# A linear-attention and gated-MLP kernel: features turned by transposing DMAs, key-value sums kept in PSUM, q and k weights read from DRAM turned

## The chip, the cores and the metric

The kernel runs on one core of one Trainium2 chip. The metric is device time in microseconds (us) of one execution; lower is better. The engines are TensorE (PE in the rows; its weight loads are PEld), VectorE (DVE), ScalarE (ACT), GpSimd (POOL) and SyncE (SP), which here only issues DMAs.

## The reference

A token matrix x of 2048 x 512 is normalised, and two branches of the normalised xn are added to x. Branch A is linear attention with 32 heads of 16 features; phi is a softmax of w_phi's product and a softmax of its negative, side by side.

```
xn = (x - mean) / sqrt(var + 1e-5)
q, k, v = split(xn @ wqkv)                       # 32 heads of 16
pq, pk = q @ w_phi, k @ w_phi                    # per head, 16 x 16
phi = concat(softmax(p), softmax(-p))            # 32 features a head, of pq and of pk
kv, z = sum_s phi_k * v, sum_s phi_k             # per head
A = ((phi_q @ kv) / (phi_q @ z + 1e-6)) @ wo
B = ((xn @ w_gate) * (xn @ w_up)) @ w_down       # inner width 1792
out = x + A + B
```

## The kernel before

Tokens are worked in 16 tiles of 128. The weights and x are loaded at the start by SP's queue, whole matrix by whole matrix (lines 347 to 364); w_phi's 16 KB come by GpSimd's queue. `wprime_steps` folds w_phi into the q and k weights: f1 turns a 128-column block of wq or wk with four TensorE transposes (matmuls by the identity, line 323, evicted by ScalarE, line 287), f2 multiplies it by the block-diagonal `wbd` that GpSimd builds (line 395).

Then three stages. **Opening**: per four tiles, normalisation statistics (DVE line 432, and nine tiny GpSimd operations for the inverse root, lines 448 to 455), per tile `emit_xn` (line 465) and `emit_xT`, four TensorE transposes. **k stage**, per tile: `k_stage1` makes k's features and v (eight matmuls of 512 columns, line 309; exponentials by ScalarE), `k_stage2` sums each head (line 499), takes reciprocals (line 504) and scales both halves (line 506, one on DVE, one on GpSimd) into an array of all 16 tiles; gate and up products of 5 of the 14 inner blocks go in between (`emit_glu_up`, 512 columns at a time). `emit_kv` then sums the key-value products over all tiles, 128 matmuls of 129 columns. **q stage**, per tile: `q_stage1` makes the features, `q_stage2a` turns them (eight TensorE transposes), multiplies them by the key-value sums (eight matmuls of 128 columns) and by z (eight of 8 columns); `q_stage2b` divides on DVE, `q_stage2b_pe` turns the result (four transposes). `final_chunks` fills in the other 9 inner blocks (256 columns at a time, lines 674, 675 and 679), the down and wo products (line 654), and adds x by a matmul with the identity.

Each operation is a step with its reads and writes; `_emit_all` orders all engines' steps by a list schedule over assumed costs, and each engine then runs its list in that order, waiting on semaphores. In these lines the q stage is paced:

```
    for t in range(NT):
        q_stage2b(t)
        if t + 2 < NT:
            q_stage1(t + 2)
        emit_c(1)
        if t + 1 < NT:
            q_stage2a(t + 1)
        emit_c(1)
        q_stage2b_pe(t)
        done_2b[0] = t
        emit_c(2)
```

Of the kernel before, what the change touches and what calls it, by code (L numbers as in the profile page):

```python
# [5 lines left out]
BF16 = mybir.dt.bfloat16  # L6
# [4 lines left out]
I32 = mybir.dt.int32  # L11
# [3 lines left out]
S_TOK = 2048  # L15
D = 512
H = 32
DH = 16
# [4 lines left out]
FT_EARLY = 5  # L23


def _ap_intervals(ap, max_n=64):
    esz = mybir.dt.size(ap.dtype)
    off = ap.offset
    pairs = [tuple(pr) for pr in list(ap.ap)[1:] if pr[1] > 1]
    inner_hi = 0  # L30
    rest = []
    for step, cnt in pairs:
        if step == 1:
            inner_hi = max(inner_hi, cnt - 1)
        else:
            rest.append((step, cnt))
    total = 1
    for step, cnt in rest:
        total *= cnt
    if total > max_n:  # L40
        lo, hi = 0, inner_hi
        for step, cnt in rest:
            if step > 0:
                hi += step * (cnt - 1)
            else:
                lo += step * (cnt - 1)
        return [((off + lo) * esz, (off + hi + 1) * esz)]
    outs = []
    for n in range(total):
        base = off  # L50
        m = n
        for step, cnt in rest:
            base += step * (m % cnt)
            m //= cnt
        outs.append((base * esz, (base + inner_hi + 1) * esz))
    return outs


class _Step:
# [3 lines left out]
    def __init__(self, eng, fn, idx, lane):  # L63
# [10 lines left out]
        self.cost = 100.0  # L74
        self.seq = 0
        self.finish = 0.0


class _Sched:

    def __init__(self, nc):
        self.nc = nc
        self.steps = []
        self.by_eng = {PE: [], ACT: [], DVE: [], POOL: [], SP: []}
        self.regions = {}
        self.dma_count = 0
        self.allow_overwrite = False

    def _overlaps(self, space, lo, hi):
        out = []  # L90
        for reg in self.regions.setdefault(space, []):
            if reg[0] < hi and lo < reg[1]:
                out.append(reg)
        return out

    def _record(self, st, reads, writes):
        deps = []
        for ap in reads:
            space = str(ap.tensor.name)
            ivs = _ap_intervals(ap)  # L100
            if space == "ps":
                ivs = sorted(set((lo // 2048 * 2048, (hi + 2047) // 2048 * 2048) for lo, hi in ivs))
            for lo, hi in ivs:
                regs = self._overlaps(space, lo, hi)
                for reg in regs:
                    if reg[2] is not None and reg[2] is not st:
                        deps.append(reg[2])
                    reg[3].append(st)
                if not regs:
                    self.regions[space].append([lo, hi, None, [st]])  # L110
        for ap in writes:
            space = str(ap.tensor.name)
            for lo, hi in _ap_intervals(ap):
                new_regions = []
                for reg in self._overlaps(space, lo, hi):
                    if reg[2] is not None and reg[2] is not st and not reg[3] and not self.allow_overwrite:
                        raise RuntimeError(
                            f"step {st.idx} ({st.eng}) overwrites unread data in {space}[{reg[0]}:{reg[1]}] "
                            f"written by step {reg[2].idx} ({reg[2].eng})")
                    if reg[2] is not None and reg[2] is not st:  # L120
                        deps.append(reg[2])
                    for r in reg[3]:
                        if r is not st:
                            deps.append(r)
                    if reg[0] < lo:
                        new_regions.append([reg[0], lo, reg[2], list(reg[3])])
                    if reg[1] > hi:
                        new_regions.append([hi, reg[1], reg[2], list(reg[3])])
                    self.regions[space].remove(reg)
                self.regions[space].extend(new_regions)  # L130
                self.regions[space].append([lo, hi, st, []])
        seen = set()
        dd = []
        for d in deps:
            if id(d) not in seen:
                seen.add(id(d))
                dd.append(d)
        st.deps = dd

    def step(self, eng, fn, reads=(), writes=(), cost=None):  # L140
        st = _Step(eng, fn, len(self.steps), eng)
        self.steps.append(st)
        self.by_eng[eng].append(st)
        reads = list(reads)
        writes = list(writes)
        self._record(st, reads, writes)
        if cost is None:
            n = 1
            for ap in writes + reads:
                try:  # L150
                    n = max(n, ap.free_size())
                except Exception:
                    pass
            if eng == ACT:
                cost = 230.0 + 0.84 * n
            elif eng == DVE:
                cost = 130.0 + 1.0 * n
            elif eng == POOL:
                cost = 250.0 + 2.2 * n
            else:  # L160
                cost = 100.0 + 0.45 * n
        st.cost = cost
        return st

    def dma(self, eng, out_ap, in_ap, is_out=False, reads=None, writes=None):
        nc = self.nc
        lane = ("dma", self.dma_count)
        self.dma_count += 1
        holder = {}

        def fn(e):
            ins = e.dma_start(out_ap, in_ap)
            return ins
# [34 lines left out]
def _build(nc, es, A_x, A_wqkv, A_w_phi, A_wo, B_w_gate, B_w_up, B_w_down, out):  # L208
# [3 lines left out]
    def alloc(name, nelem_bf16, at=None):  # L212
# [724 lines left out]
```

## Time and profile before

| | |
|---|---|
| three runs | 271.51 us (median), 270.52, 272.21 |
| profiled execution, first to last instruction | 270.5 us |
| TensorE busy | 246.2 us, 91% |
| VectorE, ScalarE, GpSimd busy | 156.2, 128.1, 53.8 us |
| DMA | 12.12 MB, most of it in the first 31 us |

The profile gives no time of its execution beside the span; the median of the runs is 1.0 us above the span. An engine's busy time counts overlapping matmuls by their modelled ends, so TensorE's share says where it had work queued, not that it ran at its best rate.

### The profile page before, as it was taken

The numbers are of one execution on the slowest core, as the hardware profiler recorded it, in microseconds if no ns is written. First come the engines' busy times: TensorE is split into PE (matmuls) and PEld (weight loads), VectorE is DVE, ScalarE is ACT, GpSimd is POOL, SyncE is SP. The second block draws the span as 40 slices with busy tenths as digits, with TensorE's granted clock in tenths as the row PEclk, the third lists the DMA queues.
The fourth block names the chain that finished last, engine by engine and source line by source line (L and its number), as shares of the span: only waits on it lengthen the run. The fifth ranks groups of instructions, "written<-read, shape, count | busy, mean of one in ns | idle before, by whom it ended". The sixth has DMA issues, their size and how long they took to land.

```text
span 270.5 us, 4879 instructions
## 1 busy us (share of the span) xinstructions
PE 246.2 (91%) x1902; PEld 156.7 (58%) x1936; DVE 156.2 (58%) x364; ACT 128.1 (47%) x261; POOL 53.8 (20%) x99
## 2 busy tenths in 40 slices
PE   0068999999999999999999999999999999999994
PEld 0046544444444587777567765775766757566661
DVE  3951699989797985787677776542232323313231
ACT  1057898646665704776665755632222313222221
POOL 4560253333442430313112131100000000000000
PEclk9999999999999999999999999999999999999999
DMA  6999300000000000000000001001001010000101
GB/s 198 351 393 381 119 0 1 2 0 0 0 0 2 0 4 2 0 2 0 22 19 2 4 1 41 0 2 39 0 2 39 2 39 0 26 15 2 39 1 39
DMA packets 9446, 12.12 MB, mean 45 GB/s; under 512 B 448, under 2 KB 8400, under 8 KB 9424
## 3 DMA queue, kind: packets, MB, share of 16 engines
q1 hardware_dynamic: 9392, 11.80, 12.6%
q8 instruction: 15, 0.25, 0.4%
q0 software_dynamic: 32, 0.02, 0.1%
q14 instruction: 7, 0.06, 0.1%
HBM read 9.72 MB, written 2.10 MB: 44 GB/s over the span
## 4 chain that ended last, share of the span: by engine, by line
PE 80%; DVE 8%; ACT 3%; DMA 3%; issue 3%; POOL 2%; DVEq 0%; POOLq 0%
PE ps L309 50%; PE ps L654 24%; PE ps L323 7%; ACT arena L287 3%; DMA arena<-in_A_w_phi_dram 3%; DVE arena L499 2%; DVE arena L506 1%; DVE arena L534 1%; DVE arena L504 1%; POOL arena L395 1%; DVE arena L465 1%; DVE arena L576 0%; DVE arena L679 0%; DVE arena L457 0%; POOL arena L449 0%
## 5 line engine op out<-in xcount | busy, mean ns | idle before, releaser
L287 ACT ACTIVATE arena<-ps 128x512 bf16<-128x512 f32 (+1 forms) x260 | 126.9, 541 | 138.9 <-PE ps L309 92.9
L309 PE MATMUL ps<-arena 128*128 128x256 bf16 (+4 forms) x1300 | 172.6, 279 | 1.6 <-ACT arena L287 0.5
L309 PEld LDWEIGHTS ps<-arena 128*128 128x128 bf16 x1312 | 109.0, 98 | 59.0 <-PE ps L309 2.2
L654 PE MATMUL ps<-arena 128*128 128x512 bf16 x282 | 77.9, 381 | 2.0 <-DVE arena L679 0.6
L679 DVE TENSOR_TENSOR arena<-ps,arena 128x256 bf16<-128x256 f32 x72 | 30.0, 416 | 55.3 <-PE ps L654 52.9
L323 PE MATMUL ps<-arena 128*128 128x128 bf16 x320 | 30.9, 240 | 17.6 <-POOL arena L450 14.9
L654 PEld LDWEIGHTS ps<-arena 128*128 128x128 bf16 x304 | 28.0, 97 | 24.4 <-PE ps L654 4.4
L323 PEld LDWEIGHTS ps<-arena 128*128 128x128 bf16 x320 | 24.4, 107 | 27.1 <-DMA arena<-in_A_wqkv_dram 14.9
L506 POOL TENSOR_TENSOR arena<-arena 128x512 bf16<-128x512 bf16 x16 | 22.6, 1413 | 34.6 <-DVE arena L504 26.3
L584 POOL TENSOR_TENSOR arena<-arena 128x512 bf16<-128x512 bf16 x16 | 16.9, 1056 | 63.0 <-DVE arena L582 47.0
L576 DVE TENSOR_REDUCE arena<-arena 128x32 f32<-128x512 bf16 x32 | 20.6, 678 | 7.3 <-ACT arena L287 7.2
L499 DVE TENSOR_REDUCE arena<-arena 128x32 f32<-128x512 bf16 x32 | 20.6, 678 | 6.0 <-ACT arena L287 6.0
L534 DVE TENSOR_TENSOR arena<-ps,arena 128x512 bf16<-128x512 f32 x20 | 13.6, 682 | 1.5 <-PE ps L309 1.4
L432 DVE BATCH_NORM_STATS2 arena<-arena 128x6 f32<-128x512 bf16 x16 | 10.5, 684 | 4.8 <-DMA arena<-in_A_x_dram 4.8
L707 DVE CAST arena<-ps 128x512 bf16<-128x512 f32 x8 | 5.5, 692 | 12.4 <-PE ps L654 12.3
L506 DVE TENSOR_TENSOR arena<-arena 128x512 bf16<-128x512 bf16 x16 | 11.6, 728 | 0.4
L465 DVE TENSOR_SCALAR arena<-arena 128x512 bf16<-128x512 bf16 x16 | 5.8, 410 | 9.8 <-PE ps L323 9.8
L621 DVE TENSOR_TENSOR arena<-ps,arena 128x512 bf16<-128x512 f32 x16 | 10.9, 682 | 0.3
L504 DVE RECIPROCAL arena<-arena 128x64 f32<-128x64 f32 x16 | 8.8, 550 | 0.4
L618 DVE SCALAR_TENSOR_TENSOR arena<-arena,ps 128x32 f32<-128x32 f32 x16 | 3.0, 188 | 10.3 <-PE ps L309 10.1
L620 DVE RECIPROCAL arena<-arena 128x32 f32<-128x32 f32 x16 | 5.6, 351 | 0.4
L581 DVE RECIPROCAL arena<-arena 128x32 f32<-128x32 f32 x16 | 5.6, 348 | 0.4
(31 smaller groups left out, 30.3 us busy)
## 6 DMA issues: line engine op xcount, KB each, us to landing
arena<-in_A_x_dram SPq DMA_DIRECT2D x4, 512.0 KB, 6.6
out_dram<-arena SPq DMA_DIRECT2D x16, 128.0 KB, 1.7
arena<-in_B_w_gate_dram SPq DMA_DIRECT2D x1, 1792.0 KB, 12.0
arena<-in_B_w_up_dram SPq DMA_DIRECT2D x1, 1792.0 KB, 15.2
arena<-in_B_w_down_dram SPq DMA_DIRECT2D x1, 1792.0 KB, 18.1
arena<-in_A_wqkv_dram SPq DMA_DIRECT2D x3, 512.0 KB, 11.2
arena<-in_A_wo_dram SPq DMA_DIRECT2D x1, 512.0 KB, 8.9
arena<-in_A_w_phi_dram POOLq DMA_DIRECT2D x1, 16.0 KB, 7.5
```

Source lines behind the costliest of these rows:

```text
L287: return e.activation(out=out_ap, in_=in_ap, func=func, scale=scale, **kw)
L309: ins = e.matmul(out_ap, lhsT=l, rhs=r, start=(i == 0), stop=(i == n - 1))
L323: ins = e.matmul(o, lhsT=l, rhs=r, start=True, stop=True)
L499: dve(lambda e, side=side: e.tensor_reduce(out=sm[:, side * 32:(side + 1) * 32], in_=ering(slot, side).rearrange("p (h f) -> p h f", f=16) ...
L504: dve(lambda e: e.reciprocal(out=rs, in_=sm), [sm], [rs])
L506: fn = (lambda e, side=side: e.tensor_tensor(out=ek_v[:, side, t, :].rearrange("p (h f) -> p h f", f=16), in0=ering(slot, side).rearrange( ...
L534: dve(lambda e: e.tensor_tensor(out=dest_ap, in0=bank(bu), in1=gring(slot), op=ALU.mult), [bank(bu), gring(slot)], [dest_ap])
L576: dve(lambda e, side=side: e.tensor_reduce(out=sm[:, side * 32:(side + 1) * 32], in_=ering(slot, side).rearrange("p (h f) -> p h f", f=16) ...
L584: pool(lambda e: e.tensor_tensor(out=enr(slot).rearrange("p (h f) -> p h f", f=16), in0=ering(slot, 1).rearrange("p (h f) -> p h f", f=16) ...
L621: dve(lambda e: e.tensor_tensor(out=oring(slot).rearrange("p (h d) -> p h d", d=16), in0=bank(bo).rearrange("p (h d) -> p h d", d=16), in1 ...
L654: return e.matmul(o, lhsT=lhsT, rhs=rhs, start=first, stop=last)
L679: dve(lambda e: e.tensor_tensor(out=h, in0=bank(bu, 256, 256), in1=g, op=ALU.mult), [bank(bu, 256, 256), g], [h])
```

## The change

The kernel is written anew around the same computation.

- q and k weights come turned from DRAM by `dma_start_transpose` on SP's queue (`load_qkT`); f1's transposes go. The fold (`w_fold`) stays. Loads are issued in smaller pieces in the order of need; w_phi is loaded by ScalarE's queue.
- The inverse root is two ScalarE operations (logarithm, exponential).
- A tile's features of both signs lie side by side, head by head (`features`). Only the negative half is scaled, by the ratio of the two sums; for k, the reciprocal of the positive sum goes into v (`v_stage`), with itself as a 17th column.
- The key-value sums stay in two PSUM banks: per tile eight matmuls of 68 columns (`kv_acc`).
- q's features are turned by one transposing DMA a tile (`q_transpose`), 128 x 1024 elements, and the attention result by another, 128 x 512, in `num_stage`, which makes numerator and denominator in eight matmuls of 68 columns.
- Gate and up products are all 512 columns wide, taken two a tile in the k loop and in the first half of the q loop. x is added on DVE.
- TensorE keeps the order of the program's text; the other engines and queues are ordered by a list schedule as before.

```
-        for jt in range(NQ):
-            def f1(jt=jt):
...
+    def load_qkT(w):
+        o, i = wT_v[:, w], A_wqkv[:, w * 512:(w + 1) * 512]
+        sc.dma(SP, lambda e: e.dma_start_transpose(o, i), [], [("wT", w)], 524288)
...
+    load_x(0, 2)
+    load_qkT(1)
+    load_x(2, 2)
...
+    def features(name, t, w):
...
+        act(e_v[:, :, 0, :], src, [("ps", b)], [(name, s, 0)], func=ACTF.Exp)
+        act(e_v[:, :, 1, :], src, [("ps", b)], [(name, s, 1)], func=ACTF.Exp, scale=-1.0)
...
+        pool(lambda e: e.tensor_tensor(out=e_v[:, :, 1, :], in0=e_v[:, :, 1, :],
+                                       in1=rat[:, :, None].to_broadcast([128, H, 16]), op=ALU.mult),
+             [(name, s, 1), ("rat", s)], [(name, s, 1)], 512)
...
+    def kv_acc(t):
...
+            for c in range(8):
+                ins = e.matmul(bank(c // 4, (c % 4) * CW, CW), lhsT=ek[:, c * 128:(c + 1) * 128],
+                               rhs=vs[:, c * CW:(c + 1) * CW], start=(t == 0 and c % 4 == 0),
+                               stop=(t == NT - 1), skip_group_check=True)
...
+    def q_transpose(t):
+        s = t % RQ
+        reads = [("eq", s, 0), ("eq", s, 1)]
+        src = sb("eq", s * 1024, 1024)
+        wk = [("wT", 0), ("wT", 1)] if t < RP else []
+        sc.dma(SP, lambda e: e.dma_start_transpose(ph_tile(t), src), reads, [("phT", t % RP)] + wk, 262144, free=wk)
...
-    def q_stage2a(t):
...
-            mm_multi(items)
-            act_op(eT_all[:, r, side * 4:(side + 1) * 4, :], bank(tb[side]).rearrange("p (c s) -> p c s", c=NQ), func=ACTF.Copy)
...
+    def num_stage(t):
...
+                ins = e.matmul(bank(c // 4, (c % 4) * CW, CW), lhsT=ph[:, c, :], rhs=kvz_v[:, c, :], start=True,
+                               stop=True)
...
+        sc.dma(SP, lambda e: e.dma_start_transpose(oT_tile(t), o_tile(t)), [("o", t % 3)], [("phT", t % RP)], 131072)
...
     for t in range(NT):
+        if t + 3 < NT:
+            features("eq", t + 3, 0)
+            q_transpose(t + 3)
+        up()
+        num_stage(t)
+        up()
+        if t >= 2:
+            out_tile(oq.pop(0))
```

How the change moves instructions, at three places. First the opening on TensorE; line 323 is before's transposes and folds; in the change, line 343 is the turning of x and line 307 the fold, `dsem2` the transposing load of wk. Before:

```order
L323 MATMUL ps<-arena 128x128 [waits sem_POOL,dsem5]
L323 MATMUL ps<-arena 128x128 x7
L323 MATMUL ps<-arena 128x128 [waits sem_ACT,sem_PE]
L323 MATMUL ps<-arena 128x128 x3
L323 MATMUL ps<-arena 128x128 [waits sem_ACT,sem_PE]
L323 MATMUL ps<-arena 128x128 x3
L323 MATMUL ps<-arena 128x128 [waits sem_POOL,sem_ACT]
```

In the change, TensorE, and below it ScalarE's list at the same place (line 237 loads w_phi, the small operations are the inverse root):

```order
L343 MATMUL ps<-arena 128x128 [waits sem_POOL,sem_DVE]
L343 MATMUL ps<-arena 128x128 x3
L343 MATMUL ps<-arena 128x128 [waits sem_DVE]
L343 MATMUL ps<-arena 128x128 x3
L307 MATMUL ps<-arena 128x128 [waits sem_ACT,sem_POOL,dsem2]
L307 MATMUL ps<-arena 128x128 x3
L307 MATMUL ps<-arena 128x128 [waits sem_ACT]
```

```order
L237 DMA arena<-in_A_w_phi_dram 128x4x16
L186 ACTIVATE arena<-arena 128x1 [waits sem_POOL,sem_DVE]
L186 ACTIVATE arena<-arena 128x1 [waits sem_DVE]
L186 ACTIVATE arena<-arena 128x1 [waits sem_ACT] x2
L186 ACTIVATE arena<-ps 128x4x128 [waits sem_PE] x2
L186 ACTIVATE arena<-arena 128x2 [waits sem_DVE]
L186 ACTIVATE arena<-ps 128x512 [waits sem_PE]
L186 ACTIVATE arena<-arena 128x2 [waits sem_ACT]
L186 ACTIVATE arena<-ps 128x512 [waits sem_PE] x3
L186 ACTIVATE arena<-ps 128x4x128 [waits sem_PE] x2
```

x's first tiles are turned ahead of the fold now, and the fold's first eviction stands behind the inverse root of tiles 2 and 3.

Second, SP's queue in the q stage: line 427 is `q_transpose`, line 457 the turning of the result, line 492 the output. Before:

```order
L172 DMA out_dram<-arena 128x512 [waits sem_ACT]
L172 DMA out_dram<-arena 128x512 [waits sem_DVE] x2
L172 DMA out_dram<-arena 128x512 [waits sem_ACT] x2
L172 DMA out_dram<-arena 128x512 [waits sem_DVE]
L172 DMA out_dram<-arena 128x512 [waits sem_ACT]
```

In the change:

```order
L427 DMA_TRANSPOSE arena<-arena 128x8x128 [waits sem_POOL,sem_ACT]
L427 DMA_TRANSPOSE arena<-arena 128x8x128 [waits dsem25,sem_POOL,sem_ACT]
L427 DMA_TRANSPOSE arena<-arena 128x8x128 [waits dsem26,sem_POOL,sem_ACT]
L457 DMA_TRANSPOSE arena<-arena 128x4x128 [waits sem_DVE]
L427 DMA_TRANSPOSE arena<-arena 128x8x128 [waits dsem27,sem_POOL]
L457 DMA_TRANSPOSE arena<-arena 128x4x128 [waits sem_DVE]
L427 DMA_TRANSPOSE arena<-arena 128x8x128 [waits dsem28,sem_POOL]
L457 DMA_TRANSPOSE arena<-arena 128x4x128 [waits sem_DVE]
L427 DMA_TRANSPOSE arena<-arena 128x8x128 [waits dsem30,sem_POOL]
L492 DMA out_dram<-arena 128x512 [waits sem_DVE]
L457 DMA_TRANSPOSE arena<-arena 128x4x128 [waits sem_DVE]
```

Each of the first eight feature transposes waits until the one ahead has landed (dsem25, 26, 27, 28, 30, ...), since all of them lie over the place of the turned weights; the queue held outputs alone before.

Third, one tile of the q stage on TensorE. Before (line 323 transposes, line 309 of 128x128 and 128x8 the products with the sums, 128x256 gate and up, 128x512 the q projection; line 654 down, wo and x):

```order
L309 MATMUL ps<-arena 128x512 [waits sem_DVE,sem_PE]
L309 MATMUL ps<-arena 128x512 x3
L323 MATMUL ps<-arena 128x128 [waits sem_ACT]
L323 MATMUL ps<-arena 128x128 x3
L323 MATMUL ps<-arena 128x128 [waits sem_POOL]
L323 MATMUL ps<-arena 128x128 x3
L309 MATMUL ps<-arena 128x256 x8
L654 MATMUL ps<-arena 128x512 [waits sem_PE,sem_DVE]
L323 MATMUL ps<-arena 128x128 [waits sem_ACT,sem_PE,sem_DVE]
L323 MATMUL ps<-arena 128x128 x3
```

In the change, a tile of the second half of the q stage (line 441 the product with the sums; `dsem44` a feature transpose, `dsem48` a result's):

```order
L441 MATMUL ps<-arena 128x68 [waits sem_DVE,dsem44]
L441 MATMUL ps<-arena 128x68 x7
L205 MATMUL ps<-arena 128x512 x14
L205 MATMUL ps<-arena 128x512 [waits dsem48]
L205 MATMUL ps<-arena 128x512 x3
L205 MATMUL ps<-arena 128x512 [waits sem_ACT]
L205 MATMUL ps<-arena 128x512 x3
```

The transposes are gone from TensorE, and it waits on two DMAs a tile in their place.

## Rows read from the trace of the kernel before

**Rows 1.** The page: busy time of the engines; share, instructions.

```profile
PE 246.2 (91%) x1902; PEld 156.7 (58%) x1936; DVE 156.2 (58%) x364; ACT 128.1 (47%) x261; POOL 53.8 (20%) x99
...
PE 80%; DVE 8%; ACT 3%; DMA 3%; issue 3%; POOL 2%; DVEq 0%; POOLq 0%
```

**Rows 2.** Chain that ended last, in order of time: start us, us, what.

```profile
1.31 7.54 DMA arena<-in_A_w_phi_dram
9.00 1.57 POOL arena L395 x4
14.89 0.62 PE ps L323 x4
...
55.54 8.79 PE ps L309 x40
...
128.78 0.45 PE ps L323 x8
...
131.82 0.63 PE ps L309 x16
...
196.19 0.87 PE ps L309 x8
...
267.48 0.69 DVE arena L707
```

**Rows 3.** The same view: four matmuls of 512 columns.

```profile
133.13 0.86 PE ps L309 x4
```

**Rows 4.** TensorE's groups up to 55.5 us, by form.

```profile
L309 PE MATMUL ps<-arena 128*128 128x512 bf16 x108 | 25.6, 379 | 0.9 <-ACT arena L287 0.5 <-PE ps L323 0.2
L323 PE MATMUL ps<-arena 128*128 128x128 bf16 x128 | 14.2, 272 | 17.5 <-POOL arena L450 14.9 <-ACT arena L287 2.6
```

**Rows 5.** Busy time in stretches: us, PE, PEld, DVE, ACT, POOL, granted clock, DMA.

```profile
0.00:10.00 10.00, 0.00 (x0) 0.00 (x0) 5.60 (x19) 1.28 (x1) 4.04 (x18) 1.00 0.77 248
...
31.00:45.00 14.00, 13.30 (x89) 6.91 (x90) 13.24 (x27) 12.98 (x26) 6.48 (x15) 1.00 0.00 1
45.00:60.00 15.00, 14.77 (x68) 6.55 (x68) 13.94 (x24) 8.97 (x17) 5.54 (x4) 1.00 0.01 1
```

**Rows 6.** Whole run by line and form: DVE, GpSimd and ScalarE operations that recur.

```profile
L287 ACT ACTIVATE arena<-ps 128x512 bf16<-128x512 f32 x188 | 101.5, 601 | 79.5 <-PE ps L309 33.5 <-PE ps L323 28.2 <-PE ps L654 15.3
...
L506 POOL TENSOR_TENSOR arena<-arena 128x512 bf16<-128x512 bf16 x16 | 22.6, 1413 | 34.6 <-DVE arena L504 26.3 <-ACT arena L287 8.4
L499 DVE TENSOR_REDUCE arena<-arena 128x32 f32<-128x512 bf16 x32 | 20.6, 678 | 6.0 <-ACT arena L287 6.0
...
L534 DVE TENSOR_TENSOR arena<-ps,arena 128x512 bf16<-128x512 f32 x20 | 13.6, 682 | 1.5 <-PE ps L309 1.4
...
L432 DVE BATCH_NORM_STATS2 arena<-arena 128x6 f32<-128x512 bf16 x16 | 10.5, 684 | 4.8 <-DMA arena<-in_A_x_dram 4.8
...
L504 DVE RECIPROCAL arena<-arena 128x64 f32<-128x64 f32 x16 | 8.8, 550 | 0.4
...
L465 DVE TENSOR_SCALAR arena<-arena 128x512 bf16<-128x512 bf16 x16 | 5.8, 410 | 9.8 <-PE ps L323 9.8
...
L581 DVE RECIPROCAL arena<-arena 128x32 f32<-128x32 f32 x16 | 5.6, 348 | 0.4
...
L582 DVE TENSOR_TENSOR arena<-arena 128x32 f32<-128x32 f32 x16 | 3.0, 188 | 0.3
```

**Rows 7.** DMA issues: out<-in, queue, count, KB each, median us to landing.

```profile
out_dram<-arena SPq DMA_DIRECT2D x16, 128.0 KB, 1.7
...
arena<-in_A_w_phi_dram POOLq DMA_DIRECT2D x1, 16.0 KB, 7.5
```

**Rows 8.** The loads of x, 512 KB each, in the tile view.

```profile
DMA to landing us min/median/max: 3.5/6.6/9.5
```

More of the change, by code (lines that the diff above doesn't have):

```diff
@@ L17 @@
 H = 32
-DH = 16
 FF = 1792
@@ L22 @@
 NF = FF // 128
[L23 to L56, printed above, removed]
+NSG = 4
+FSL = 256
+HC = 17
+CW = 4 * HC
 class _Step:
@@ L73, in __init__ @@
         self.is_out = False
-        self.cost = 100.0
+        self.cost = cost
         self.seq = 0
@@ L79, with __init__ @@
 class _Sched:
-    def __init__(self, nc):
-        self.nc = nc
+    def __init__(self):
         self.steps = []
-        self.by_eng = {PE: [], ACT: [], DVE: [], POOL: [], SP: []}
-        self.regions = {}
+        self.writer = {}
+        self.readers = {}
         self.dma_count = 0
[L87 to L138, printed above, removed]
@@ L142, in step @@
+    def step(self, eng, fn, reads, writes, cost):
+        st = _Step(eng, fn, len(self.steps), eng, cost)
         self.steps.append(st)
-        self.by_eng[eng].append(st)
-        reads = list(reads)
-        writes = list(writes)
         self._record(st, reads, writes)
[L147 to L161, printed above, removed]
@@ L366, in c_fn @@
+    load_gu(SP, 0)
+    load_x(4, 4)
+    load_gu(SP, 1)
+    load_gu(SP, 2)
+    load_x(8, 4)
+    load_qkT(0)
+    load_gu(SP, 3)
+    load_x(12, 4)
+    for s in range(4, FF // FSL):
+        load_gu(SP, s)
+    load_w(SP, wd_v, B_w_down.rearrange("(f p) j -> p f j", p=128), "wd", 1835008)
+    load_w(SP, wo_v, A_wo.rearrange("(q p) j -> p q j", p=128), "wo", 524288)
     def c_fn(e):
@@ L791, in _build @@
[L791 to L813 removed]
+    lnv = sbf("lnv", 0, NT)
@@ new lines, in _build, with next_up, up @@
+    ups = [(ft, sg) for sg in range(NSG) for ft in range(NF)]
+    def next_up(pairs):
+        if ups:
+            ft, sg = ups.pop(0)
+            up_unit(ft, sg, pairs)
+    PAIRS = [(4, 5), (6, 7)]
+    def up(n=1):
+        for _ in range(n):
+            if ups:
+                up_unit(*ups.pop(0), PAIRS)
+    ln_stats(0, 1)
+    ln_apply(0)
+    ln_stats(1, 1)
+    ln_apply(1)
+    ln_stats(2, 2)
+    for t in range(2, 4):
+        ln_apply(t)
+    x_transpose(0)
+    x_transpose(1)
+    for dt in range(NQ):
+        w_fold(1, dt)
@@ new lines, in _build @@
+    x_transpose(2)
+    x_transpose(3)
+    wq_steps = [lambda dt=dt: w_fold(0, dt) for dt in range(NQ)]
+    for t in range(NT + 2):
+        if t < NT:
+            features("ek", t, 1)
+        if t in (0, 2, 4):
+            ln_stats(4 + 2 * t, 4)
+        up()
+        if 2 * t + 4 < NT:
+            ln_apply(2 * t + 4)
+            x_transpose(2 * t + 4)
+        elif wq_steps and t >= 6:
+            wq_steps.pop(0)()
+        if 0 <= t - 1 < NT:
+            v_stage(t - 1)
+        up()
+        if 2 * t + 5 < NT:
+            ln_apply(2 * t + 5)
+            x_transpose(2 * t + 5)
+        elif wq_steps and t >= 6:
+            wq_steps.pop(0)()
+        if t >= 2:
+            kv_acc(t - 2)
+        if t >= NT - 1:
+            features("eq", t - NT + 1, 0)
+            q_transpose(t - NT + 1)
+            up()
@@ new lines, in _build @@
+    kv_finish()
+    up()
+    oq = list(range(NT))
+    for t in range(NT):
+        if t + 3 < NT:
+            features("eq", t + 3, 0)
+            q_transpose(t + 3)
+        up()
+        num_stage(t)
+        up()
+        if t >= 2:
+            out_tile(oq.pop(0))
+    up(len(ups))
+    while oq:
+        out_tile(oq.pop(0))
+    n_sems = sc.dma_count
+    eng_sems = {e: es.enter_context(nc.semaphore(f"sem_{e}")) for e in (PE, ACT, DVE, POOL)}
+    dma_sems = [es.enter_context(nc.semaphore(f"dsem{i}")) for i in range(n_sems)]
```

861 lines of the change are left out of this document (312 added, 549 removed).

## The prediction

> **What bounds the kernel now.** I read the page first: TensorE is busy 246.2 of 270.5 us and holds 80% of the chain that ended last [rows 1]. The chain in order of time then shows where it isn't TensorE: up to its first matmul at 14.89 us, and in pieces until 55.54 us; from there to the last eviction at 267.48 us it is nearly all TensorE [rows 2]. So the question is how much TensorE work goes, and what stops TensorE meanwhile.
>
> Busy time overstates matmuls, so I price them by the spacing inside unbroken pieces of the chain. Four matmuls of 512 columns take 0.86 us [rows 3] and eight of 256 columns 0.87 [rows 2]; I use 0.2175 us and 0.109 each. Eight transposes of 128 columns take 0.45 us, 0.056 each; eight products of 128 columns with eight of 8 columns take 0.63 us [rows 2], so one of 8 columns takes (0.63 - 0.45) / 8 = 0.0225.
>
> Before, the program has 656 matmuls of 512 columns (142.7 us), 576 of 256 (62.8), 320 transposes and folds (17.9), 128 + 128 of 128 and 129 columns (14.4) and 128 of 8 (2.9): **240.7 us**. Up to 55.54 us, 108 of 512 and 128 of 128 columns are recorded [rows 4], 23.5 + 7.2 = 30.7 us of work in 55.54 - 14.89 = 40.65: **10.0 us of waiting in the opening** after the first matmul. DVE was busy 13.24 of 14 and 13.94 of 15 us there [rows 5]. From 55.54 to 267.48 it is 211.9 us for 210.0 of work: **1.9 us of waiting**. The tail behind the last matmul is 270.5 - 267.5 = **3.0**. With the 14.9 ahead this is 14.9 + 10.0 + 240.7 + 1.9 + 3.0 = 270.5, the span. The median of the runs is 1.0 above the span, and I add that at the end.
>
> **The change, part by part.** *TensorE's work.* Gone: 16 x 12 transposes of q's features and results and 32 of the weights (224 x 0.056 = 12.5 us), and 16 additions of x (3.5). The key-value products were 128 x 0.056 = 7.2 us, the products with the sums and z 7.2 + 2.9 = 10.1; each is 128 matmuls of 68 columns now. No row has 68 columns; between 0.0225 (8 columns) and 0.056 (128) I take the proportion to the columns, 68 / 128 x 0.056 = 0.030, and a little for the issue, 0.031: 4.0 us each, ends 2.9 and 7.2. Gate and up at 512 columns for 256 cost the same (288 x 0.2175 = 62.6 against 62.8). New total: 928 x 0.2175 + 96 x 0.056 + 256 x 0.031 = 201.8 + 5.4 + 7.9 = **215.1 us, 25.6 less**. All of it lay on the path; it comes off the end if nothing takes its place.
>
> *The opening.* TensorE's list starts with tiles 0 and 1 of x, then the fold, which waits for the transposing load of wk and for GpSimd's `wbd`. The first load of x lands 3.5 us after its issue [rows 8], and statistics (0.68), two small ScalarE operations and the scaling (0.41) [rows 6] put x's first transpose at about 6.5 us. The wk load has no row: the trace has no transposing DMA. Its least price is a plain 512 KB load, 3.5 us. The dearest load for its size is w_phi's in runs of 16 elements, 7.5 us for 16 KB [rows 7]; I take it, since a turned load breaks up its rows too, which lands wk at about 1.3 + 7.5 = 8.8 us. By the same price on ScalarE's queue, behind the table load that ends at about 2.1 us, w_phi lands at 9.6, and four GpSimd products (1.57 us [rows 2]) finish `wbd` at 11.2. The fold then needs four evictions of 0.6 us [rows 6], and tiles 2 and 3 of x another: dense work starts at about 14.7. The bounds: with both loads at 3.5 us the inverse root of tiles 2 and 3, which stands ahead of the fold's evictions on ScalarE, holds, and work is dense from 11.5; with a wk load twice as dear (15 us) from 21. Ahead of the dense part lie 1.8 us of work (16 transposes, 16 folds), so the loss is 14.7 - 1.8 = **12.9**, where before lost 14.9 and part of the 10.0.
>
> *The first six rounds of the k loop* also turn two tiles of x each. TensorE's work per round: 24 matmuls of 512 columns, 8 transposes, 8 of 68 columns, 5.2 + 0.45 + 0.25 = 5.9 us. DVE's: a sum over 1024 elements (2 x 0.678), reciprocal 0.55, ratio 0.19, v 0.68, two gate products 1.36, and 2 x (0.68 + 0.16 + 0.41) of normalisation: 6.6 us of busy time [rows 6], starts overlapping by some 0.06 each. DVE and TensorE are level there, so I charge 0.7 x 6 = **4.0 us** of waiting, ends 0 and the opening's 10.0. From round 6 DVE has 4.1 us against 5.4, and costs nothing. GpSimd's product of 1.41 us a tile [rows 6] lies under the 5.4; ScalarE's two exponentials, two gate copies and two evictions (3.6 us) as well.
>
> *The q loop.* A round with gate and up products is 38 x 0.2175 + 0.25 = 8.5 us of TensorE, eight times; without them 22 x 0.2175 + 0.25 = 5.0, eight times. A tile's chain is exponentials 1.2, sum 1.36, reciprocal 0.35, ratio 0.19, GpSimd 1.41, some 5 us with handoffs, then the transposing DMA, then TensorE, three rounds later: 15 us at the least, so a DMA of up to 10 us is hidden. The result's transpose has two rounds. What isn't hidden is the queue's time if the transposes run one after another: TensorE waits if the two of a tile take over 8.5, or 5.0, us. SP's first eight feature transposes wait for each other's landing, and behind such a wait stand the result's transpose and the outputs. The bounds per transpose are 1.7 us (a plain 128 KB store, issue to landing) and 7.5 (w_phi) [rows 7]: 3.4 to 15 us a tile. I take the lower side, some 2 us each, because the code names runs of 128 elements on both sides and a source on the chip, nearer to the store's 512 than to w_phi's 16: **0** on the path. Steady waiting stays at **1.9**, the tail (eviction, store) at **3.0**.
>
> **Two rules against this.** The trace does eight transposes by TensorE in 0.45 us [rows 2]. The Trainium skill (VectorE: DVE Perf Modes, The three transpose paths) gives 390 ns for one by TensorE, seven times the row's 56, and 1309 ns by the transposing DMA; by that, an estimate, 12 blocks a tile are 15.7 us, and the sum would be that of the first rival. The Trainium skill (Advanced Engine Details and Errata, X-Bar Transpose (TRN2)) says that such DMAs are as fast as regular ones; that would leave the sum as it is. No run here shows either yet.
>
> **The sum.** 12.9 + 215.1 + 4.0 + 1.9 + 3.0 = 236.9 us of span, and with the 1.0 about **238 us**. With the early opening and no DVE waiting, 9.7 + 215.1 + 1.9 + 3.0 + 1.0 = 230.7; with the late one, 244.
>
> **Rivals.** *The transposes become the bound.* At 7.5 us each, one after another, a tile takes 15: the q loop takes 16 x 15 = 240 for 8 x 8.5 + 8 x 5.0 = 108, so 238 + 132 = **370 us, slower than before**. It decides from 16s - 108 = 33.5, s = 8.8 us a tile. For it: SP waits for landings in the first half, and nothing in the trace shows a cheap transpose. Against it: 384 KB a tile is three of the stores that land in 1.7 us. Here belongs the 1309 ns rule. Chance 0.18, with 0.03 more for a price between that just eats the gain. *They bind the second half alone*, at 7.5 us a tile (two at half w_phi's price): 8 x (7.5 - 5.0) = 20 us, **258**. Chance 0.15. *DVE becomes the bound of the k loop*, its list in an order that TensorE, now in fixed order, waits on: the opening's 10.0 us for my 4.0, and half of that again in the rounds behind, **247**. For it: DVE was the chain there before. Against: after round 6 it has room. Chance 0.10.
>
> **How the numbers follow.** The forecast (231 to 246) has 0.54. The rivals at 247 and 258 are faster than before too; the range runs from 231 to 262 and leaves out the first rival and what lies between. A measurement of this kernel, whose runs lie within 0.4% of their median, tells 1% from no change. Faster by over 1%: 0.54 + 0.10 + 0.15 = 0.79; within 1%: 0.03; slower: 0.18.
>
> **What would show it.** Right: matmuls of 512 columns still spaced 0.2175; first matmul near 6.5 us and unbroken work from 14 to 15; transposing DMAs landing within 5 us; TensorE waiting in the q loop on no DMA. Wrong: TensorE idle ahead of line 441 or the wo matmuls with a transposing DMA as the releaser (first two rivals), idle ahead of line 205 with DVE as the releaser between 15 and 110 us (third), or a fold that starts past 15 us.

## The result, and the profile after

The changed kernel takes **237.62 us** (median of 4 runs, 236.47 to 238.51) where the kernel before took 271.68 beside it: a ratio of **0.8735**, 95% interval 0.8695 to 0.8776. The forecast was 238, in a range of 231 to 262. The profiled execution has a span of 236.8 us and took 238.51, so what lies around the span is 1.7 us; the 1.0 in the prediction was the distance of before's span to the median of its runs. Of the four executions, the one with a mean granted clock of 1.000 has a span of 234.7 us and the three with 0.993 have 235.8 to 236.8; the profiled one is the longest.

The page of the changed kernel, for [rows 1]: busy time of the engines, then the chain's shares.

```profile
PE 218.5 (92%) x1255; PEld 105.5 (45%) x1280; DVE 146.0 (62%) x282; ACT 82.7 (35%) x157; POOL 42.8 (18%) x65
...
PE 89%; DVE 3%; DMA 2%; issue 2%; ACT 1%; SPq 1%
```

TensorE still bounds the kernel, with 27.7 us less of busy time (25 of 1280 matmul records are missing); ScalarE lost 45.4 us, most of it (56 evictions of 0.6 us, 33.6) since it no longer evicts what TensorE turned in the q stage and of the weights. The same chain in order of time, for [rows 2, 3] (start us, us, what):

```profile
1.31 2.60 SPq L241
3.97 4.13 DMA arena<-in_A_x_dram
...
8.73 0.41 DVE arena L333
9.19 0.62 PE ps L343 x4
...
14.51 1.90 PE ps L205 x4
...
20.12 0.40 PE ps L343 x4
...
32.98 0.40 PE ps L343 x4
33.38 4.28 PE ps L205 x12
...
37.88 0.26 PE ps L400 x8
...
72.97 5.18 PE ps L205 x24
...
194.54 0.26 PE ps L441 x8
...
199.54 0.26 PE ps L441 x8
...
233.07 0.82 PE ps L205 x3
233.91 0.69 DVE arena L490
```

Line 343 turns x, 205 holds every matmul of 512 columns, 400 the key-value products, 441 the products with the sums. From these rows the prices are: 5.18 / 24 = 0.2158 us for 512 columns and 0.26 / 8 = 0.032 for 68. With 0.055 for a transpose, the program's 928, 256 and 96 of them are 200.3 + 8.2 + 5.3 = **213.8 us** of work.

Where that work didn't run, or ran slower than priced: dense work starts at 14.51, behind 1.8 us of transposes and folds (at 0.055 each), a loss of **12.7**. From there to the first key-value product at 37.88 lie 68 matmuls and 24 transposes, 16.0 us of work in 23.37: **7.4 lost**. From 37.88 to the end of the last matmul, 233.89, are 196.0 us for the remaining 213.8 - 1.8 - 16.0 = 196.0: **nothing lost**, through 200 us and all 32 transposing DMAs. Tail: 236.8 - 233.9 = **2.9**. Sum: 12.7 + 213.8 + 7.4 + 2.9 = 236.8.

TensorE's waits (waiting line, releaser: us in total, times, longest):

```profile
PE ps L343 <- DVE arena L333: 13.1, 3, 9.2
PE ps L307 <- ACT arena L186: 0.6, 2, 0.4
PE ps L343 <- ACT arena L186: 0.2, 1, 0.2
```

All are in the opening: 9.2 us before the first transpose, and two more waits on DVE's scaling of x (line 333), 3.9 together, ahead of 20.12 and 32.98. None is on a DMA. The stretches, for [rows 5] (start:end, length; busy us of PE, PEld, DVE, ACT, POOL; granted clock, DMA share, GB/s):

```profile
15.00:20.00 5.00, 3.50 (x12) 1.15 (x10) 3.21 (x8) 1.97 (x6) 0.11 (x1) 1.00 1.12 228
20.00:31.00 11.00, 10.46 (x58) 5.11 (x60) 10.97 (x25) 7.09 (x14) 2.78 (x4) 1.00 1.10 316
31.00:45.00 14.00, 11.97 (x73) 5.89 (x75) 10.78 (x24) 5.63 (x12) 2.92 (x4) 0.88 0.31 100
...
190.00:225.00 35.00, 34.79 (x208) 16.80 (x210) 22.60 (x46) 5.00 (x10) 5.27 (x5) 1.00 0.49 97
```

DVE is full from 20 to 31 us. From 31 to 45 the granted clock is 0.88, partly the 1.2 GHz level: in the trace's clock records it falls at 34.1 us, 1.1 us behind the end of the second wait, and is back at full at 37.5, and twelve matmuls took 4.28 us for 2.59. The row for 15 to 20 us says 1.00, but the clock records of this trace begin only at 17.03 us, and the view prints 1.00 where it has none. Ahead of 17.03 TensorE ran at the lower level from its first matmul on: transposes start 0.107 us apart (0.055 later), matmuls of 512 columns 0.427 (0.216 later), which is 1.2 columns a ns for 2.4. The first six of 512 columns, in the timeline:

```profile
14.51 2.70 PE L205 MATMUL ps<-arena 128*128 128x512 bf16 x6
```

The trace of the kernel before has the same start: its clock records begin at 27.24 us, and the 76 matmuls recorded up to there, all of 128 columns, lie 0.107 us apart inside their runs (PE is the second column):

```profile
14.89:27.24 12.35, 9.57 (x76) 7.37 (x78) 3.41 (x11) 8.85 (x17) 3.40 (x17) 1.00 1.05 389
```

The DMA issues, for [rows 7] (median us from issue to landing), and below them the source view of the feature transposes (line 427) and the result's (line 457): how long each holds SP's sequencer (ns, least/median/most), and its landing.

```profile
out_dram<-arena SPq DMA_DIRECT2D x16, 128.0 KB, 1.7
...
arena<-in_A_wqkv_dram SPq DMA_TRANSPOSE x2, 5.8
arena<-in_A_w_phi_dram ACTq DMA_DIRECT2D x1, 16.0 KB, 3.3
```

```profile
L427 SPq DMA_TRANSPOSE arena<-arena x16: 1233/1246/2119, 117.4 to 214.8; - x16
...
DMA to landing us min/median/max: 3.1/3.2/4.7
```

```profile
L457 SPq DMA_TRANSPOSE arena<-arena x16: 1189/1196/1271, 135.2 to 223.9; - x16
...
DMA to landing us min/median/max: 2.4/2.4/4.2
```

A tile's two transposes land in 3.2 + 2.4 us, not in 2 + 2; the three rounds ahead still cover them. Their sum, 5.6, is over a round of 5.0 (194.54 to 199.54), yet TensorE didn't wait. The two holds, 1.2 us each, sum to 2.4: either the landings overlap, or something else paces the queue. The experiments settle which.

### The profile page after: what moved, and what is told of

It is laid out like the page before. It is cut to its first block, busy times and chain, and to the rows that moved or that the text cites. A ratio compares the mean times of both kernels' runs of the same rounds, so it can differ in the third digit from the quotient of the medians.

```text
span 236.8 us, 3283 instructions
## 1 busy us (share of the span) xinstructions
PE 218.5 (92%) x1255; PEld 105.5 (45%) x1280; DVE 146.0 (62%) x282; ACT 82.7 (35%) x157; POOL 42.8 (18%) x65
## 3 DMA queue, kind: packets, MB, share of 16 engines
q1 hardware_dynamic: 44448, 18.09, 33.6%
## 4 chain that ended last, share of the span: by engine, by line
PE 89%; DVE 3%; DMA 2%; issue 2%; ACT 1%; SPq 1%
PE ps L205 83%; PE ps L343 2%; DMA arena<-in_A_x_dram 2%; PE ps L441 2%; PE ps L400 2%; ACT arena L186 1%; SPq L241 1%; PE ps L307 1%; DVE arena L475 1%; DVE arena L324 1%; DVE arena L365 0%; DVE arena L369 0%; DVE arena L333 0%; DVE arena L490 0%; SPq L226 0%
## 5 line engine op out<-in xcount | busy, mean ns | idle before, releaser
L205 PE MATMUL ps<-arena 128*128 128x512 bf16 x903 | 207.7, 383 | 1.4
L205 PEld LDWEIGHTS ps<-arena 128*128 128x128 bf16 x928 | 88.5, 98 | 101.9 <-issue 3.3
L186 ACT ACTIVATE arena<-ps 128x512 bf16<-128x512 f32 (+1 forms) x144 | 79.6, 597 | 124.0 <-PE ps L205 108.2
L365 DVE TENSOR_REDUCE arena<-arena 128x64 f32<-128x1024 bf16 x32 | 38.9, 1216 | 33.9 <-ACT arena L186 33.9
L375 POOL TENSOR_TENSOR arena<-arena 128x512 bf16<-128x512 bf16 x32 | 34.0, 1061 | 90.6 <-DVE arena L373 86.1
L475 DVE TENSOR_TENSOR arena<-ps,arena 128x512 bf16<-128x512 f32 x56 | 38.4, 685 | 12.8 <-PE ps L205 12.8
L490 DVE TENSOR_TENSOR arena<-ps,arena 128x512 bf16<-128x512 f32 x16 | 11.1, 691 | 30.0 <-PE ps L205 30.0
L387 POOL CAST arena<-arena 128x32 bf16<-128x32 f32 x16 | 5.2, 326 | 78.5 <-DVE arena L369 75.0
L343 PE MATMUL ps<-arena 128*128 128x128 bf16 x64 | 6.9, 242 | 13.4 <-DVE arena L333 13.1
L343 PEld LDWEIGHTS ps<-arena 128*128 128x128 bf16 x64 | 5.1, 108 | 17.4 <-DVE arena L333 14.1
L453 DVE TENSOR_TENSOR arena<-ps,arena 128x512 bf16<-128x512 f32 x16 | 11.1, 691 | 0.5
L388 DVE TENSOR_TENSOR arena<-ps,arena 128x512 bf16<-128x512 f32 x16 | 10.2, 636 | 0.1
L441 PEld LDWEIGHTS ps<-arena 128*128 128x128 bf16 x128 | 6.2, 97 | 3.8
L400 PEld LDWEIGHTS ps<-arena 128*128 128x128 bf16 x128 | 5.9, 97 | 2.4
L441 PE MATMUL ps<-arena 128*128 128x68 bf16 x128 | 6.7, 194 | 0.0
L400 PE MATMUL ps<-arena 128*128 128x68 bf16 x128 | 6.7, 194 | 0.0
L373 DVE TENSOR_TENSOR arena<-arena 128x32 f32<-128x32 f32 x32 | 5.9, 184 | 0.2
```

The costliest lines, as they stand in the source:

```text
L186: return sc.step(ACT, lambda e: e.activation(out=out_ap, in_=in_ap, func=func, scale=scale, **kw), reads, writes, 130.0 + 0.833 * n)
L205: ins = e.matmul(out_ap, lhsT=l, rhs=r, start=start and i == 0, stop=stop and i == npair - 1, **kw)
L343: ins = e.transpose(bank16(b, q * 128, 128), xn_tile(t)[:, q * 128:(q + 1) * 128], ident)
L365: dve(lambda e: e.tensor_reduce(out=sm, in_=e_v, axis=AX.X, op=ALU.add), [(name, s, 0), (name, s, 1)], [("sums", sr)], 1024)
L375: pool(lambda e: e.tensor_tensor(out=e_v[:, :, 1, :], in0=e_v[:, :, 1, :], in1=rat[:, :, None].to_broadcast([128, H, 16]), op=ALU.mult), [ ...
L388: dve(lambda e: e.tensor_tensor(out=vs_tile(t)[:, :, 0:16], in0=bank(b).rearrange("p (h f) -> p h f", h=H), in1=rp.unsqueeze(2).to_broadca ...
```

## The experiments

Times are medians of several executions; each ratio is to the kernel before, timed beside it (271.1 to 271.6 us). Where the time matters to 1%, I compare with 237.62 and, for the three kernels that ran beside it, with the repeat of the change.

**The transposes back on TensorE.** Features and results are turned by TensorE and evicted by ScalarE in place of the 32 DMAs; all else is the change.

```
-        sc.dma(SP, lambda e: e.dma_start_transpose(ph_tile(t), src), reads, ...
+            for c in range(8):
+                ins = e.transpose(bank16(3, c * 128, 128), src[:, c * 128:(c + 1) * 128], ident)
...
+        act(ph_tile(t), bank16(3, 0, 1024).rearrange("p (c s) -> p c s", c=8), [("ps", 3)], ...
...
-        sc.dma(SP, lambda e: e.dma_start_transpose(oT_tile(t), o_tile(t)), ...
+    def o_transpose(t):
...
+                ins = e.transpose(bank16(b, q * 128, 128), o_tile(t)[:, q * 128:(q + 1) * 128], ident)
```

> The changed kernel with q's features and the results turned by TensorE again (192 transposes of 128 columns, evicted by ScalarE) in place of the 32 transposing DMAs; all else stays. My theory, that these DMAs are wholly hidden and the work that left TensorE is the gain: 192 x 0.055 = 10.6 us more, 248 us, up to 3 us above that for handoffs through PSUM. Rival, that the DMAs hold TensorE up somewhere in the q stage: less than 10.6 us more, down to no change at 238. Rival, that they don't matter because the q stage is bound elsewhere: 238.

Measured: **249.9 us** (248.97 to 250.46), ratio 0.9205 (0.9168 to 0.9241); 12.3 over the change. The 192 transposes are 192 x 0.055 = 10.6 us of work; the other 1.7 fits waits for handoffs (1.5 us of its waits are in lines that don't wait in the change). So the DMAs take their work off the path in full, and about 12 of the change's 34 us come from them. No run takes back the narrower products with the key-value sums (17.3 us of work before, 8.2 now) or the 16 additions of x (3.5); their part stands by count and spacing alone.

**Each transposing DMA of the q stage twice, and three times.** The copies go to a place that nothing reads, so the outputs stay as they are.

```
         sc.dma(SP, lambda e: e.dma_start_transpose(ph_tile(t), src), reads, [("phT", t % RP)] + wk, 262144, free=wk)
+        for _ in range(1):   # range(2) in the second kernel
...
+            sc.dma(SP, lambda e, d=d: e.dma_start_transpose(d, src), reads, [("dum", i)], 262144, free=[("dum", i)])
```

(and the same behind the result's transpose.)

> Each of the 32 transposing DMAs of the q stage is issued twice, the second time into an unused place. Theory: SyncE holds about 1.22 us per transpose and 0.34 per store, so a tile takes 4 x 1.22 + 0.34 = 5.2 us of its queue against rounds of 8.5 and 5.0 us: 238 to 242 us. Rival, that the transposes are at the edge already (landing 3.2 + 2.4 us a tile one after another, 11.2 us when doubled): 16 x 11.2 - 108 = 71 us more, 309.

> Each transposing DMA of the q stage is issued three times, twice into unused places. Theory: 6 x 1.22 + 0.34 = 7.7 us of SyncE's queue a tile, over the 5.0 us of the last eight rounds and under the 8.5 of the first: 8 x 2.7 = 21 us more, 259, which is the prediction's formula with its second rival's place; more if the DMA engines themselves fill up. Rival by landing times, one after another: 16.8 us a tile, 161 us more, 398.

Measured: **243.65 us** (242.40 to 244.34), ratio 0.8986 (0.8948 to 0.9025); and **267.13** (266.39 to 267.83), ratio 0.9842 (0.9801 to 0.9883). Both are above the first theory's numbers and far below the rivals' 309 and 398. One tile of SP's list in the kernel with three, in its last rounds (line 430 the feature transpose, 435 its two copies, 465 the result's, 470 its copies, 506 the output), and the landings from the chain:

```profile
215.19 1.23 SPq L430 DMA_TRANSPOSE arena<-arena  x1
216.46 2.72 SPq L435 DMA_TRANSPOSE arena<-arena  x2
219.22 1.28 SPq L465 DMA_TRANSPOSE arena<-arena  x1
220.54 2.57 SPq L470 DMA_TRANSPOSE arena<-arena  x2
223.16 0.58 SPq L506 DMA_DIRECT2D out_dram<-arena  x1
```

```profile
215.19 3.21 DMA arena<-arena
...
223.79 3.21 DMA arena<-arena
...
232.40 3.23 DMA arena<-arena
```

The transpose whose landing TensorE waits for is issued every 8.6 us (215.19, 223.79, 232.40). That is SP's list of one tile, seven issues one after another: 1.23 + 2.72 + 1.28 + 2.57 + 0.58, with gaps of 0.04 between them. From 133 us on the queue never stands idle for as much as 0.5 us. The landing times, 3 x (3.2 + 2.4) = 16.8, don't set it: they overlap. By the formula of the first rival with s = 8.6, the loss is 8 x (8.6 - 8.5) + 8 x (8.6 - 5.0) = 29.6, and 267.13 - 237.62 = 29.5. On TensorE the loss shows as 20.6 us of waits on transposes and, at granted clocks of 0.95 from 190 to 225 us and 0.80 from 225 to 260, 8.8 us of slower running, 29.4 together; the queue paces these rounds either way.

With two of each, five issues hold SP for 1.24 + 1.34 + 1.19 + 1.27 + 0.58 by the medians of its trace, 5.9 with the gaps, a loss of 8 x 0.9 = 7; measured 6.0. That agreement is loose: TensorE keeps rounds of 5.0 us up to 207.5, and from 182 us to there SP's queue stands idle four times, for up to 1.8 us. Behind that TensorE waits 3.5 us for transposes, and a granted clock of 0.66 from 218 to 223 us costs 1.7. So it is the kernel with three that shows the form of the rival to be right, with the **hold of SP's sequencer** as its s, **some 3 us a tile in the change**, where 5.0 is the point from which the second half waits.

**q and k weights loaded plainly.** They land as they lie in DRAM and are turned by 32 TensorE transposes, as before; the rest is the change.

```
-        sc.dma(SP, lambda e: e.dma_start_transpose(o, i), [], [("wT", w)], 524288)
+        load_w(SP, wqk_v[:, w], A_wqkv[:, w * 512:(w + 1) * 512].rearrange("(q p) j -> p q j", p=128), ("wqk", w), 524288)
...
+                ins = e.transpose(bank16(b, dt * 128, 128), wqk_v[:, w, dt, jt * 128:(jt + 1) * 128], ident)
...
+        act(wT_v[:, w, jt, :], bank16(b, 0, 512), [("ps", b)], [("wT", w, jt)])
```

> The changed kernel with the q and k weights loaded plainly and turned by TensorE, 32 transposes and eight evictions, as before; all else stays. Theory: SyncE is free 2 us earlier, so tiles 2 and 3 of x land earlier by 2 us, but four turns of wk with their evictions (about 2.6 us) come into the opening's chain, and 16 more transposes of wq later (0.9 us): 238 to 240 us. Rival, that the turned load is what delays the opening: 2 us less, 236. Rival, that the turned weights carry a good part of the gain: over 242.

Measured: **239.36 us** (238.17 to 239.73), ratio 0.8812 (0.8776 to 0.8848): 1.7 over the change. That is the price of 32 transposes (1.8), but the trace adds it up otherwise. Its dense work starts 2.1 us later than 14.51, behind four turns of wk and their evictions:

```profile
16.57 3.94 PE ps L206 x12
```

The wait of 1.62 us that follows in the change isn't there, and wq's 16 transposes are 0.9: 1.4 together. The intervals of the two ratios just meet, so the turned weights are worth about 0.7%, and little more is sure than that they don't cost.

**The change again**, beside the next three. Its expectation:

> The changed kernel as it is, beside the next three on the same chip: 237.6 us by every theory.

Measured: **236.90 us** (235.63 to 238.61), ratio 0.8734 (0.8693 to 0.8774), the first ratio once more. Its chain has the low rate in the first matmuls alone:

```profile
14.28 5.01 PE ps L205 x12
...
34.02 2.59 PE ps L205 x12
```

Here the first twelve matmuls took 5.01 us, nearly twice 2.59: they ran at the lower level up to 18.84 us, where the clock records of this trace begin, in place of 17.03. The twelve behind the second wait, 2.30 us long as in the result's trace, ran at full rate.

**x's second load ahead of the turned wk**, since the chain of the change runs through SP's 2.60 us hold to the load of tiles 2 and 3.

```
     load_x(0, 2)
-    load_qkT(1)
     load_x(2, 2)
+    load_qkT(1)
```

> Tiles 2 and 3 of x are loaded ahead of the turned wk instead of behind it. Theory: the opening hangs on that load (issued at 3.97 us, behind 2.6 us of SyncE's hold, landed at 8.1), because VectorE's list has their statistics ahead of the scaling of tiles 0 and 1; it lands near 5 us, the first transpose starts near 6.3 and unbroken work near 12: 2 to 3 us less, 235. Rival, that the landing of wk or of w_phi sets it, as the prediction had it: no change.

Measured: **235.76 us** (234.95 to 236.65), ratio 0.8693 (0.866 to 0.8725): 1.1 under the repeat, half of what I expected, and the intervals overlap. Compared at like granted clock they come apart: at 1.000 the spans are 233.2 to 233.6 us here and 233.9 to 235.8 in the repeat, at 0.993 they are 234.4 to 234.9 and 235.6 to 236.9. Dense work starts where I expected it, 2.6 us earlier than 14.51, but the next wait grew from 1.62 to 2.49 us (timeline; the wait stands in brackets):

```profile
11.88 3.89 PE L205 MATMUL ps<-arena 128*128 128x512 bf16 x12
18.27 0.40 PE L343 MATMUL ps<-arena 128*128 128x128 bf16 x4 [2.49 <-DVE arena L333]
```

The chain moved on to the next load, of tiles 4 to 7, and their statistics on DVE:

```profile
6.21 6.76 DMA arena<-in_A_x_dram
12.99 1.29 DVE arena L324 x2
```

**x's scaling on GpSimd** from tile 4 on, alone and together with the earlier load.

```
+        if t >= 4:
+            pool(f, r, wr, 512, 1.6)
+        else:
+            dve(f, r, wr, 512, 0.27)
```

> The scaling of x's tiles from the fifth on is done by GpSimd instead of VectorE. Theory: TensorE's waits of 1.62 and 2.30 us in the first rounds, and the lower clock behind the second (12 matmuls in 4.28 us for 2.59), come from VectorE's list, in which that scaling stands behind k's sums: 3 to 5 us less, 234. Rival, that x's loads set these waits: no change. Rival, that GpSimd is slower at it than the wait was long: up to 3 us more.

> Both edits, tiles 2 and 3 of x ahead of wk and the scaling on GpSimd. Theory: the two gains lie one behind the other in the opening and add: 5 to 8 us less, 231. Rival, that an earlier start only meets a longer wait for VectorE: no more than the better of the two.

Measured: **236.36 us** (235.90 to 237.72), ratio 0.8717 (0.8686 to 0.8749), and **236.04** (235.15 to 237.27), ratio 0.8703 (0.8669 to 0.8737): neither is told from the repeat, and the gain expected of each isn't there. In the first, TensorE waits for GpSimd in DVE's place (chain, then waits):

```profile
15.93 1.86 ACT arena L186 x5
...
18.00 2.08 POOL arena L333
```

```profile
PE ps L347 <- POOL arena L333: 4.2, 2, 2.5
```

GpSimd takes 2.08 us for what DVE does in 0.41 (at 8.73 in the chain after). It starts when ScalarE has ended its work of 15.93 to 17.79, with the inverse root of these tiles in it, so DVE's list wasn't all that stood ahead of the scaling. In the second, the chain goes through SP, whose hold for the turned wq delays the load of the last four tiles of x:

```profile
12.23 4.87 SPq L241
...
18.32 5.13 DMA arena<-in_A_x_dram
```

**Gate and up in halves of 256 columns**, two matmuls for each of 512.

```
-        mm(bank(bg), [(wg_v[:, q, fs], xnT(q, sg * 512, 512)) for q in range(NQ)], ...
+        for hb in range(2):
+            mm(bank(bg, hb * 256, 256), [(wg_v[:, q, fs], xnT(q, sg * 512 + hb * 256, 256)) for q in range(NQ)], ...
```

> The changed kernel with each gate and up product of 512 columns made in two of 256, 448 matmuls and weight loads more. The prediction put the wider products at nothing (0.109 us for 256 columns, 0.2175 for 512), so: within 1 us of 237. Rival, that a part of the gain came from half as many weight loads (0.1 us each): 10 us or more above.

Measured: **239.14 us** (238.01 to 239.39), ratio 0.8804 (0.8779 to 0.8829), 1.5 over the change where I expected at most 1. One round of the k loop, to be set against 5.18 us for 24:

```profile
67.27 5.22 PE ps L205 x40
```

0.04 us a round, over the 28 rounds' worth of gate and up products (56 in all, two a round), is 1.1 us of the 1.5; the rest has no row. The prediction had the two widths level (62.6 for 62.8). This kernel halves all 14 inner blocks, of which the change had widened 9, so the wide products are worth about 1 us of the change's 34: the gain isn't there.

**All loads of x ahead**, wq's turned load last before the down and wo weights, statistics four tiles earlier. This joins what the three opening runs showed: each load of x had stood behind a hold or a weight.

```
     load_x(0, 2)
-    load_qkT(1)
     load_x(2, 2)
+    load_qkT(1)
+    load_x(4, 4)
     load_w(SP, wv_v, ...
     load_gu(SP, 0)
-    load_x(4, 4)
-    load_gu(SP, 1)
-    load_gu(SP, 2)
     load_x(8, 4)
-    load_qkT(0)
-    load_gu(SP, 3)
+    load_gu(SP, 1)
     load_x(12, 4)
...
+    load_qkT(0)
...
+    ln_stats(4, 4)
...
-        if t in (0, 2, 4):
-            ln_stats(4 + 2 * t, 4)
+        if t in (0, 2):
+            ln_stats(8 + 2 * t, 4)
```

> All of x is loaded ahead of most weights (tiles 0 to 3, turned wk, 4 to 7, wv, first gate and up slices, 8 to 11, second slices, 12 to 15), the turned wq goes behind the gate and up weights, and each group's statistics come one step earlier. Theory: the opening is a chain of x's loads on SyncE's queue with VectorE behind them, and the turned loads' holds of 2.6 and 4.9 us stand in it; VectorE has time before unbroken work starts: that starts near 11.5 in place of 14.3 and the wait of round 0 shrinks: 3 to 5 us less, 233. Rival, that VectorE's own order is the bound in the first rounds whatever is loaded: 1 us less, as with tiles 2 and 3 alone. Rival, that later weights now arrive late: slower.

Measured: **234.66 us** (233.43 to 235.46), ratio 0.8645 (0.8618 to 0.8672), the only version whose interval lies below the change's. Its chain, and the stretch from 31 to 45 us:

```profile
6.89 7.78 DMA arena<-in_A_x_dram
...
20.03 0.40 PE ps L341 x4
...
33.77 0.25 PE ps L398 x8
```

```profile
31.00:45.00 14.00, 14.00 (x92) 7.14 (x91) 10.58 (x21) 7.84 (x14) 3.16 (x6) 1.00 0.33 111
```

TensorE is unbroken from 20.03 on, at the full clock; the first key-value product comes at 33.77, against 37.88 after: 4.1 us, the difference of the spans (236.8 - 232.7). The gain isn't where I expected it. Dense work starts at 13.45, not near 11.5, behind a new wait (timeline):

```profile
12.15 1.03 PE L341 MATMUL ps<-arena 128*128 128x128 bf16 x8 [1.39 <-DVE arena L331]
13.45 5.15 PE L205 MATMUL ps<-arena 128*128 128x512 bf16 x12 [0.26 <-ACT arena L186]
```

These first twelve run at the lower clock, 5.15 us for 3.99 in the result's trace, which takes back the 1.1 us of earlier start. The wait ahead of 20.03 is left, 1.44 us for 1.62: tiles 8 to 11 land at 14.67, and DVE's list has their statistics ahead of the scaling that TensorE waits for. What is gone is the second wait, 2.30 us, and the low clock behind it, 1.7. The latter isn't in every execution of the change, and the medians are 3.0 us apart, or 2.2 against the repeat.

## Why the prediction was right

**TensorE's work was three quarters of the gain, and the opening most of the rest**, about as forecast. The spacing of 512 columns is 0.2158 for 0.2175 (1.6 us over 928), and 0.216 in before's trace too, so before is priced anew with 0.2158 and 0.055: 239.0 us of work, and 239.0 - 213.8 = 25.2 less, where 25.6 was predicted. Ahead, between and behind, TensorE lost 31.5 us before (270.5 - 239.0) and 23.0 after: 8.5 less, where 14.9 + 10.0 + 1.9 against 12.9 + 4.0 + 1.9 promised 8.0. The 68 columns cost 0.032 for 0.031. The value between the rows of 8 and of 128 columns was good to 3%.

**The transposing DMAs are hidden**, but the margin was not where the text put it. It took 2 us a landing and asked for s under 5.0 in the second half; by landings s would be 5.6, over the point, and the second rival would have been due a loss of 8 x 0.6 = 5 us. What the queue repeats is the sequencer's hold, and landings overlap: s is 1.25 + 1.20 + 0.34 for the store, and gaps, some 3 us. The kernel with three of each shows it by its rounds. So the first two rivals named the right condition with the wrong price, and the term 0 was right, though not for the reason given, a landing of some 2 us.

The change's 0.2 us for each further block bears on the two rules weighed there. A 128 x 512 transpose (4 blocks) lands in 2.4 us and a 128 x 1024 (8 blocks) in 3.2: 0.2 us a block above some 1.6. The Trainium skill (VectorE: DVE Perf Modes, The three transpose paths) gives 1309 ns for one block by DMA and 390 by TensorE; the trace agrees with neither as a price per block (0.2 more for each; 0.055 in a run of transposes). The Trainium skill (Advanced Engine Details and Errata, X-Bar Transpose (TRN2)) has the transposing DMA as fast as a regular one; here 128 KB turned land in 2.4 us and 128 KB stored plainly in 1.7, so at this size the trace doesn't quite agree, and SP is held 1.20 us for the one and 0.34 for the other.

**The opening was right in size and wrong in cause**, which is luck. Dense work starts at 14.51 for the 14.7 predicted. But the reason given, w_phi's 7.5 us landing and so `wbd` at 11.2, fell: on ScalarE's queue w_phi landed in 3.3 us, and the turned wk in 4.7 for the 7.5 it was priced at. The first transpose of x, put at 6.5, came at 9.19. The step that failed is the one that let x's statistics and scaling of tiles 0 and 1 follow their own load: the load of tiles 2 and 3 stood behind SP's hold of 2.60 us, and DVE's list has statistics of those tiles ahead of the scaling. Two errors of opposite sign met. The kernel with that load ahead shows the hold's part: its first transpose comes at 6.57 us, as predicted, and its dense work at 11.88. It gave only 1.1 us, since the next load took its place.

**The first rounds were mis-sized**: 4.0 us predicted, 7.4 lost. Waits on DVE were 3.9 of it, the size forecast, but not its form: not 0.7 us in each of six rounds but two waits, at tiles 4 and 8, the first of their groups of four, whose statistics stand ahead in DVE's list. The rest is TensorE at the lower level: 12 matmuls in 4.28 us for 2.59 behind the second wait, 1.7, and the first 12 in 14.51 to 18.5 (20.12 less the wait's 1.6) for 2.59, 1.4. No term of the sum had it. The prediction could have met it in before's trace: of the 10.0 us that it called waiting in the opening, 76 x (0.107 - 0.056) = 3.9 are matmuls at the lower level.

In return the steady 1.9 us fell to nothing (0.9 of it was the price of 0.2175 over the 548 matmuls behind 55.54 us), and the tail was 2.9 for 3.0; the errors are +1.3 (work), +0.2, -3.4, +1.9, +0.1, together +0.1. That they cancel is luck, and so is the last step: the profiled execution is the longest of the four, the median of their spans is near 235.9, 1.0 under the 236.9 forecast, and 1.7 us lie around the span where 1.0 was added.

**The third rival**, DVE as the bound of the k loop, holds only for its first rounds. Behind 37.88 TensorE waits on DVE nowhere. Its sign, idle time ahead of line 205, wouldn't have caught even these: both waits stand ahead of line 343, the turning of x.

What stays open: why the clock falls once more at 34.1 us in the result's trace and not in the repeat's, with a second wait of 2.30 us in both. In the profiled execution of the kernel with all loads of x ahead that wait and that fall are both absent, but two of its five executions have a granted clock of 0.993, so the wait alone isn't shown to be the cause.

## What to carry to other kernels

Ask of a DMA that replaces work on TensorE two things apart: its landing, which a few rounds of other work cover, and how long its issue holds the queue's sequencer, which adds up tile by tile and stands ahead of every load and store behind it. A total that comes out right says little of its terms: the opening agreed to 0.2 us with a cause that wasn't there, and only the chain's own rows showed what to move. When the bound engine has lost its excess work, what is left is its feed: the order of the first loads and of the statistics was worth 2 to 3 us here, more than the turned weights. And a price read in the middle of a run doesn't hold at its start: up to 17 us here a matmul took twice the time that the sum gave it.

## What the runs showed that I had not expected

- A transposing DMA between places on the chip holds SP for 1.2 us whether it has 128 x 512 or 128 x 1024 elements (1.27 to 1.34 for the copies); one of 512 x 512 from DRAM holds it for 2.6 us on an idle queue and 4.87 among other loads. A plain store of 128 KB holds it 0.34, and 0.58 in the kernels with copies.
- w_phi's 16 KB in short runs, 7.5 us on GpSimd's queue [rows 7], took 3.3 on ScalarE's. The surroundings changed as well, so the queue alone isn't shown to be the reason.
- GpSimd scales a 128 x 512 tile with two values per partition in 2.08 us, DVE in 0.41.
- A granted clock of 1.00 in a view can mean that there is no record. Twelve matmuls took 5.01 us at 14.28, at half rate, where the view prints 1.00; the clock records of that trace begin at 18.84 us, and from there on the spacing is that of the full clock. At the start, the spacing of matmuls shows the level.
